# A convolution and a gated feed-forward on one core: the output projection with Wo stationary in column tiles, and the work that moves with it

## The chip, the cores and the metric

The kernel runs on one core of a Trainium2 chip. The metric is the device time of one execution in microseconds (us), as the median of several runs. Engines go by the names of the profile: PE is TensorE (matmuls; PEld its weight loads), DVE VectorE, ACT ScalarE, POOL GpSimd, SP the engine that issues DMAs here.

## The reference

The input x has 8 batches of 4096 tokens with 192 channels; `weight` has 8 heads of 7 taps. What is computed, cut to what matters:

```python
w = softmax(weight)                        # per head, over its 7 taps
x_pad = 6 zero tokens in front of each batch of x
attn[b, s, ch] = sum_k w[head(ch), k] * x_pad[b, s + k, ch]   # head(ch) = ch // 24
t = attn.reshape(32768, 192)
out = (relu(t @ w_gate) * (t @ w_val)) @ w_out                # 192 -> 1536 -> 192
```

So a causal convolution of 7 taps per channel, then a gated feed-forward. The output is 32768 x 192 in fp32; inside, the kernel works in fp16 with fp32 sums.

## The kernel before

The tokens are cut into 16 units. A unit is 1024 tokens of one batch and the same 1024 of the batch four further on, side by side as two streams (`st`), so 2048 tokens. The convolution's result of a unit is `xc`: channels on partitions (64 per stream, in 3 chunks `c`), tokens along the row, fp16.

Each turn `u` of the main loop has two stages on TensorE.

- Stage A, `gate_val` (L431), called for two windows of 512 tokens. For each of 12 slices `f` of 128 hidden channels: 6 matmuls with Wg and 6 with Wv (L444), 64 rows each, the two streams in two halves of the array's rows, 512 tokens moving. ScalarE turns the first sum into `gr` with relu (L453), VectorE multiplies it with the second out of PSUM into `hT` (L454), hidden channels on partitions.
- Stage B, `project` (L457), four times (window and stream). hT is the stationary operand, 128 tokens at a time, and Wo moves: 4 x 12 matmuls of 192 columns (L464) give 512 tokens with tokens on partitions. ScalarE copies them to `out_s` (L475), and SP stores them (L476, 384 KB).

PSUM is a rotation of four tiles `ps` of two banks each, shared by both stages: gate and value of a slice take one each, a projection takes one.

The convolution of units 0 and 1 is done by TensorE (L277, L302). For all others it runs two units ahead, on the other engines, in stage B and the following stage A. GpSimd loads x (`lane_load`, L353) and copies it in another order (`lane_turn`, L372); nine transposing DMAs on SP (L375) make `x_r`, channels on partitions. Then a unit's 1024 tokens are split in two lanes:

- VectorE's lane, 576 tokens: ScalarE makes tap 0's product `acc` (L408); VectorE adds the other six taps in 18 steps (`lane_rest`, L420), each `x_r * tap + acc`, into `xc`.
- GpSimd's lane, 448 tokens: the products of 7 taps in 3 chunks go to `prods`. ScalarE makes 16 of the 21 (L391), VectorE five after its own lane (L393, seven for unit 2). The list of VectorE's ends with chunk 2 of tap 1. GpSimd sums them in six adds over all three chunks (`add`, L397), tap 1 first; the last writes `xc`.

The order is written out by hand (`manual_schedule`): every engine runs its instructions in the order of the program. In GpSimd's queue the main loop puts, for turn `u`: the add of tap 1 for unit `u+1`, the copies for unit `u+2`, the loads for unit `u+3`, the other adds for unit `u+1`. In ScalarE's and VectorE's, stage A's work comes first, then the lanes of unit `u+2` (ScalarE's products between the evictions, four ahead of each `project`). Turn 1 is different: it also loads unit 3 and does the adds of taps 2 and 3 ahead of the copies. Turns 14 and 15 have no lanes left to start.

Of the kernel before, what the change touches and what calls it, by code (L numbers as in the profile page):

```python
# [8 lines left out]
FP = mybir.dt.float32  # L9
F16 = mybir.dt.float16  # L10
# [5 lines left out]
def kernel(  # L16
# [12 lines left out]
    nc = tc.nc  # L29

    B, S, D = x.shape
    H, KW = weight.shape
# [3 lines left out]
    NB = B // 2  # L36
    NCH = D // 64
    NBLK = D // 32
    NFF = DFF // 128
    WIN = 512  # L40
    NWIN = S // WIN
    SUB = 112
    VECTOR = [
        [(0, 5), (1, 5), (2, 5), (0, 4), (1, 4), (2, 4), (2, 1)],
        [(0, 5), (1, 5), (2, 5), (0, 6), (2, 1)],
    ]
    GSUB = 5


    UNIT = 2 * WIN  # L50
    NUNIT = NB * S // UNIT
    HALO = 64
    LDVE, LPOOL = 576, 448
    TILES = (UNIT + 2 * HALO) // 128
    TDVE = (LDVE + HALO) // 128
    GROUPS = [(0, [WIN * w + SUB * j for j in range(GSUB)]) for w in range(2)]
# [2 lines left out]

    ctx.enter_context(tc.manual_schedule())  # L60
    const = ctx.enter_context(tc.tile_pool(name="const", bufs=1))
    xpool = ctx.enter_context(tc.tile_pool(name="xpool", bufs=3))
    epool = ctx.enter_context(tc.tile_pool(name="epool", bufs=1))
    rpool = ctx.enter_context(tc.tile_pool(name="rpool", bufs=2))
    apool = ctx.enter_context(tc.tile_pool(name="apool", bufs=1))
    ypool = ctx.enter_context(tc.tile_pool(name="ypool", bufs=2))
    xcpool = ctx.enter_context(tc.tile_pool(name="xcpool", bufs=3))
    hpool = ctx.enter_context(tc.tile_pool(name="hpool", bufs=2))
    gpool = ctx.enter_context(tc.tile_pool(name="gpool", bufs=3))
    opool = ctx.enter_context(tc.tile_pool(name="opool", bufs=3))  # L70
    psum = ctx.enter_context(tc.tile_pool(name="psum", bufs=4, space=bass.MemoryType.PSUM))


    def load_x(g):


        bp, toks = GROUPS[g]
        xt = xpool.tile([128, GSUB, 2, D], F16, name="x_h")
        if toks[0] == 0:
            nc.vector.memset(xt[0:32, 0, :, :], 0.0)  # L80
        for st in range(2):
            b = bp + NB * st
            jj = int(toks[0] == 0)
            last = toks[-1] == S - SUB or toks[-1] - toks[-2] != SUB
            n_full = len(toks) - jj - int(last)
            lo = toks[jj] - PAD
            src = bass.AP(
                tensor=x.tensor,
                offset=x.offset + (b * S + lo) * D,
                ap=[[D, 128], [SUB * D, n_full], [1, D]],  # L90
            )
            nc.gpsimd.dma_start(out=xt[:, jj : jj + n_full, st, :], in_=src)  # L92
            if last:
                nc.gpsimd.dma_start(
                    out=xt[0 : SUB + PAD, len(toks) - 1, st, :],
                    in_=x[b, toks[-1] - PAD : toks[-1] + SUB, :],
                )
        for st in range(2 * int(toks[0] == 0)):
            nc.gpsimd.dma_start(
                out=xt[PAD:128, 0, st, :], in_=x[bp + NB * st, 0 : 128 - PAD, :]  # L100
            )
        return xt
# [6 lines left out]
    for half, eng in ((0, nc.sync), (1, nc.scalar)):  # L109
        eng.dma_start(  # L110
            out=wr[64 * half : 64 * half + 64],
# [12 lines left out]
    ps = psum.tile([128, 2, 512], FP, name="ps")  # L124
    for n in range(16):
        nc.tensor.matmul(  # L126
            out=ps[:, n % 2, :], lhsT=zeros[:, 0:128], rhs=zeros[:], start=True, stop=True
# [92 lines left out]
    w0 = we[:, 0:1, 0:1]  # L220
# [71 lines left out]
    def conv(g):  # L292


        xt = xts.pop(g)
        bp, toks = GROUPS[g]
        n = len(toks)
        rows = SUB + PAD
        W = 2 * n * G
        pair = [psum.tile([128, 2, 512], FP, name="ps") for _ in range(2)]  # L300
        for h, (t, bank, slot) in PLACE.items():
            nc.tensor.matmul(  # L302
                out=pair[t][0:SUB, bank, W * slot : W * (slot + 1)],
                lhsT=band(h),
                rhs=xt[0:rows, 0:n, :, G * h : G * (h + 1)],
                start=True,
                stop=True,
                skip_group_check=True,
            )
        y = ypool.tile([128, GSUB, NCH, 2, 64], F16, name="y")  # L310

        def move(copy, t, bank, i0, step_in, c, r0, step_out, width):
            src = pair[t][0:SUB, bank, 0 : 2 * W]
            dst = y[0:SUB, 0:n, 0, :, 0:1]
            copy(
                out=bass.AP(
                    tensor=dst.tensor,
                    offset=dst.offset + 128 * c + r0,
                    ap=[dst.ap[0], [step_out, 2], [NCH * 128, n], [64, 2], [1, width]],
                ),  # L320
                in_=bass.AP(
                    tensor=src.tensor,
                    offset=src.offset + i0,
                    ap=[src.ap[0], [W + step_in, 2], [2 * G, n], [G, 2], [1, width]],
                ),
            )

        move(nc.scalar.copy, 0, 0, 0, 0, 0, 0, G, G)
        move(nc.scalar.copy, 0, 1, 0, 0, 1, 8, G, G)
        move(nc.scalar.copy, 1, 0, 0, 0, 2, 16, G, G)  # L330
        move(nc.scalar.copy, 1, 1, 0, 8, 0, 48, 2 * 128 - 48, 16)
        move(nc.scalar.copy, 1, 1, 16, -16, 1, 0, 56, 8)
        for jj, t in enumerate(toks):
            nc.sync.dma_start_transpose(
                out=xc[1][:, :, t - UNIT : t - UNIT + SUB],
                in_=y[0:SUB, jj].rearrange("p c s r -> p (c s r)"),
            )
# [47 lines left out]
        return xrs[u][:, c, o : o + LDVE]  # L385

    def product(engine, u, c, k):
        out = prods[u][:, k, c, :]
        in_, scale = shifted(u, c, k, 1), tap[:, c, k : k + 1]
        if engine is nc.scalar:  # L390
            engine.activation(out=out, in_=in_, func=ACTF.Copy, scale=scale)  # L391
        else:
            engine.tensor_scalar(out=out, in0=in_, scalar1=scale, scalar2=None, op0=ALU.mult)  # L393

    def add(u, k):
        pr = prods[u]
        nc.gpsimd.tensor_tensor(  # L397
            out=pr[:, 0] if k < KW - 1 else xc[u][:, :, LDVE:UNIT],
            in0=pr[:, 0],
            in1=pr[:, k],  # L400
            op=ALU.add,
        )

    def lane_first(u):
        accs[u] = apool.tile([128, NCH, LDVE], FP, name="acc")
        xc[u] = xcpool.tile([128, NCH, UNIT], F16, name="xc")
        for c in range(NCH):
            nc.scalar.activation(  # L408
                out=accs[u][:, c, :],
                in_=shifted(u, c, 0, 0),  # L410
                func=ACTF.Copy,
                scale=tap[:, c, 0:1],
            )
        prods[u] = apool.tile([128, KW, NCH, LPOOL], FP, name="prods")

    def lane_rest(u):
        acc = accs.pop(u)
        for k in range(1, KW):
            for c in range(NCH):
                nc.vector.scalar_tensor_tensor(  # L420
                    out=xc[u][:, c, 0:LDVE] if k == KW - 1 else acc[:, c, :],
                    in0=shifted(u, c, k, 0),
                    scalar=tap[:, c, k : k + 1],
                    in1=acc[:, c, :],
                    op0=ALU.mult,
                    op1=ALU.add,
                )
        for c, k in VECTOR[u > 2]:
            product(nc.vector, u, c, k)

    def gate_val(u, w):  # L431
        h = hpool.tile([128, NFF, 2, WIN], F16, name="hT")
# [21 lines left out]
            nc.vector.tensor_tensor(out=h[:, f], in0=gr[:], in1=pss[1][:], op=ALU.mult)  # L454
        return h

    def project(bp, w, h, st, final):  # L457
        parts = [range(4)] if not final else [range(2), range(2, 3), range(3, 4)]
        row0 = (bp + NB * st) * S + WIN * w
        for n, qs in enumerate(parts):  # L460
            ps = psum.tile([128, 2, 512], FP, name="ps")
            for i, q in enumerate(qs):
                for f in range(NFF):
# [4 lines left out]
                        start=(f == 0),  # L468
                        stop=(f == NFF - 1),
                    )  # L470
            os_ = opool.tile([128, 2, 2 * D], FP, name="out_s")
            k = len(qs)
            a, m = (k + 1) // 2, min(k, 2) * D
            copy = nc.vector.tensor_copy if n == 1 else nc.scalar.copy
            copy(out=os_[:, 0:a, 0:m], in_=ps[:, 0:a, 0:m])  # L475
            (nc.scalar if n == 2 else nc.sync).dma_start(  # L476
                out=out[row0 + 128 * qs[0] : row0 + 128 * (qs[0] + k), :].rearrange(
                    "(q p) d -> p q d", p=128
                ),
                in_=os_[:, 0:a, 0:m].rearrange("p a (b d) -> p (a b) d", d=D)  # L480
                if k == 4
                else os_[:, 0, 0:m].rearrange("p (b d) -> p b d", d=D),
            )


# [3 lines left out]
    for u in range(NUNIT):  # L489
# [20 lines left out]
            xc[1] = xcpool.tile([128, NCH, UNIT], F16, name="xc")  # L510
            conv(2)
        del xc[u]
        work = [[] for _ in range(4)]
        if u + 2 < NUNIT:
            lane_first(u + 2)
            lane_rest(u + 2)
            todo = [(c, k) for k in (0, 1, 2, 3, 4, 6) for c in range(NCH)]
            todo = [ck for ck in todo if ck not in VECTOR[u > 0]]
            work = [todo[4 * i : 4 * i + 4] for i in range(4)]
        bp, w0 = u * UNIT // S, u * UNIT % S // WIN  # L520
        for i in range(4):
            for c, k in work[i]:
                product(nc.scalar, u + 2, c, k)
            project(bp, w0 + i // 2, hs[i // 2], i % 2, u == NUNIT - 1 and i == 3)
            if u == 0 and i == 0:
                conv(3)


# [28 lines left out]
```

## Time and profile before

| | |
|---|---|
| Median of 3 runs | 776.64 us (776.43 to 776.93) |
| Span of the profiled execution, first to last instruction | 774.5 us |
| Busy: PE, DVE, ACT, POOL | 765.4, 688.0, 602.3, 371.8 us |
| Granted TensorE clock | 1.000 |
| Stage A and stage B of a steady unit | 31.19 and 15.95 us |
| hT (L454) | 384 x 1221 ns |
| VectorE's lane steps (L420) | 252 x 811 ns |
| GpSimd's adds (L397) | 84 x 3.03 us |
| ScalarE's products (L391), evictions (L475) | 222 x 660 ns, 63 x 794 ns |

The durations come from one profiled execution, whose own time is its span and what lies around it. A duration is from an instruction's start to its end; neighbours on one engine overlap by some tens of nanoseconds, so their starts lie closer together than their durations say.

### The profile page before, as it was taken

Reading aid. Unit: us, or ns where it says so; the run is one execution under the profiler, and the core shown is the slowest. Engines: PE = TensorE matmul, PEld = TensorE weight load, DVE = VectorE, ACT = ScalarE, POOL = GpSimd, SP = SyncE. Lnnn points to the kernel's source line nnn. Section 1 sums busy time; section 2 is a strip of 40 time slices with the busy share of each in tenths; the row PEclk is TensorE's granted clock in tenths of the full one; section 3 lists DMA queues with packets and bytes.
Section 4 is the critical chain, followed back from the end, with each engine's and each line's share of the span. In section 5 each row is a group of like instructions: output and inputs, shape, how many; then the busy total and the mean of one; then the engine's idle time right before and its main releaser. Section 6 shows DMA issues by size and latency. Waiting matters only on the chain.

```text
span 774.5 us, 19025 instructions
## 1 busy us (share of the span) xinstructions
PE 765.4 (99%) x7952; PEld 505.7 (65%) x7952; DVE 688.0 (89%) x738; ACT 602.3 (78%) x735; POOL 371.8 (48%) x215
## 2 busy tenths in 40 slices
PE   7999999999999999999999999999999999999998
PEld 3586584855748567484764847558485674857648
DVE  6889999999999899999999999999998999986491
ACT  4798887878878787787878878788787877885572
POOL 9605929175390844809256191752908446090000
PEclk9999999999999999999999999999999999999999
DMA  9947828162291812817046281542718322100102
GB/s 113 139 69 142 90 83 93 42 100 36 82 93 60 94 24 87 87 62 114 21 89 65 84 90 42 93 42 83 92 47 93 38 87 42 63 22 22 62 1 83
DMA packets 132569, 55.62 MB, mean 72 GB/s; under 512 B 98180, under 2 KB 132484, under 8 KB 132484
## 3 DMA queue, kind: packets, MB, share of 16 engines
q1 hardware_dynamic: 90466, 38.35, 23.7%
q0 software_dynamic: 41808, 15.97, 20.4%
q8 instruction: 62, 1.02, 0.6%
q14 instruction: 23, 0.19, 0.1%
q10 hardware_dynamic: 210, 0.10, 0.0%
HBM read 31.93 MB, written 25.17 MB: 74 GB/s over the span
## 4 chain that ended last, share of the span: by engine, by line
PE 97%; DVE 1%; ACT 1%; DMA 1%; issue 1%; ACTq 0%; DVEq 0%
PE ps L444 64%; PE ps L464 33%; DMA wr<-in_weight_dram 1%; DVE hT L454 0%; ACT gr L453 0%; PE ps L302 0%; PE ps L277 0%; ACT prods L391 0%; DVE band L240 0%; DVE prod L221 0%; DVE blk L229 0%; DVE xc L287 0%; ACT out_s L475 0%; ACT we L184 0%; DVE we L181 0%
## 5 line engine op out<-in xcount | busy, mean ns | idle before, releaser
L454 DVE TENSOR_TENSOR hT<-gr,ps 128x1024 f16<-128x1024 f16 x384 | 468.6, 1221 | 62.9 <-ACT gr L453 33.6
L453 ACT ACTIVATE gr<-ps 128x1024 f16<-128x1024 f32 x384 | 392.8, 1023 | 102.9 <-PE ps L444 102.9
L397 POOL TENSOR_TENSOR prods<-prods 128x1344 f32<-128x1344 f32 x70 | 212.3, 3033 | 315.1 <-DVE prods L393 311.7
L444 PE MATMUL ps<-xc,Wv 64*128 64x512 f16 x2304 | 314.0, 376 | 1.4 <-issue 1.3
L444 PE MATMUL ps<-xc,Wg 64*128 64x512 f16 x2304 | 313.9, 376 | 0.5 <-DVE xc L287 0.3
L464 PEld LDWEIGHTS <-hT 128*128 128x128 f16 x3072 | 252.7, 98 | 6.4 <-issue 6.4
L464 PE MATMUL ps<-Wo,hT 128*128 128x192 f16 x3072 | 256.4, 246 | 0.0
L444 PEld LDWEIGHTS <-Wv 64*128 64x128 f16 x2304 | 132.0, 94 | 119.2 <-issue 2.9
L444 PEld LDWEIGHTS <-Wg 64*128 64x128 f16 x2304 | 115.2, 94 | 131.6 <-issue 3.1
L420 DVE SCALAR_TENSOR_TENSOR acc<-x_r,tap,acc 128x576 f32<-128x576 f16 x210 | 154.3, 811 | 1.8 <-ACT acc L408 1.8
L391 ACT ACTIVATE prods<-x_r,tap 128x448 f32<-128x448 f16 x222 | 130.1, 660 | 0.0
L475 ACT COPY out_s<-ps 128x768 f32<-128x768 f32 (+1 forms) x65 | 50.8, 782 | 58.3 <-PE ps L464 44.2
L353 POOL DMA_DIRECT2D x_e<-in_x_dram x56 | 45.1, 817 | 3.5 <-POOL x_p L372 2.4
L372 POOL COPY x_p<-x_e 128x1728 f16<-128x1728 f16 x28 | 44.8, 1632 | 3.2 <-DMA x_e<-in_x_dram 3.2
L397 POOL TENSOR_TENSOR xc<-prods 128x1344 f16<-128x1344 f32 x14 | 42.4, 3029 | 1.1
L420 DVE SCALAR_TENSOR_TENSOR xc<-x_r,tap,acc 128x576 f16<-128x576 f16 x42 | 31.8, 811 | 0.0
L408 ACT ACTIVATE acc<-x_r,tap 128x576 f32<-128x576 f16 x42 | 29.3, 763 | 0.0
L393 DVE TENSOR_SCALAR prods<-x_r,tap 128x448 f32<-128x448 f16 x72 | 27.3, 448 | 0.0
L475 DVE COPY out_s<-ps 128x192 f32<-128x192 f32 x1 | 0.4, 358 | 13.4 <-PE ps L464 13.4
L92 POOL DMA_DIRECT2D x_h<-in_x_dram x8 | 6.7, 843 | 0.8 <-POOLq L541 0.8
L126 PE MATMUL ps<-zeros 128*128 128x512 f16 x16 | 5.0, 482 | 1.5 <-DVE zeros L123 1.5
L277 PE MATMUL ps<-band,x_h 118*32 118x112 f16 (+7 forms) x240 | 3.5, 209 | 2.7 <-ACT band L242 2.6
(40 smaller groups left out, 49.9 us busy)
## 6 DMA issues: line engine op xcount, KB each, us to landing
out_dram<-out_s SPq DMA_DIRECT2D x63, 384.0 KB
x_e<-in_x_dram POOLq DMA_DIRECT2D x34, 192.0 KB, 6.3
x_e<-in_x_dram POOLq DMA_DIRECT2D x22, 240.0 KB, 6.2
x_r<-x_p SPq DMA_TRANSPOSE x126
x_h<-in_x_dram POOLq DMA_DIRECT2D x4, 240.0 KB, 5.7
x_h<-in_x_dram POOLq DMA_DIRECT2D x4, 192.0 KB, 5.2
Wo<-in_moe_w_out_dram POOLq DMA_DIRECT2D x1, 576.0 KB, 8.9
Wg<-in_moe_w_gate_dram POOLq DMA_DIRECT2D x3, 144.0 KB, 4.1
```

Source lines behind the costliest of these rows:

```text
L353: nc.gpsimd.dma_start(out=xe[:, j : j + n, st, :, :].rearrange("p j c r -> p j (c r)"), in_=bass.AP(tensor=x.tensor, offset=x.offset + (b ...
L372: nc.gpsimd.tensor_copy(out=xp[:, :, :, st, :], in_=xe[:, :, st, :, :])
L391: engine.activation(out=out, in_=in_, func=ACTF.Copy, scale=scale)
L393: engine.tensor_scalar(out=out, in0=in_, scalar1=scale, scalar2=None, op0=ALU.mult)
L397: nc.gpsimd.tensor_tensor(out=pr[:, 0] if k < KW - 1 else xc[u][:, :, LDVE:UNIT], in0=pr[:, 0], in1=pr[:, k], op=ALU.add,)
L408: nc.scalar.activation(out=accs[u][:, c, :], in_=shifted(u, c, 0, 0), func=ACTF.Copy, scale=tap[:, c, 0:1],)
L420: nc.vector.scalar_tensor_tensor(out=xc[u][:, c, 0:LDVE] if k == KW - 1 else acc[:, c, :], in0=shifted(u, c, k, 0), scalar=tap[:, c, k : k ...
L444: nc.tensor.matmul(out=pss[i][:, st, :], lhsT=W[64 * st : 64 * st + 64, c, 128 * f : 128 * (f + 1)], rhs=xcb[64 * st : 64 * st + 64, c, WI ...
L453: nc.scalar.activation(out=gr[:], in_=pss[0][:], func=ACTF.Relu)
L454: nc.vector.tensor_tensor(out=h[:, f], in0=gr[:], in1=pss[1][:], op=ALU.mult)
L464: nc.tensor.matmul(out=ps[:, i // 2, D * (i % 2) : D * (i % 2) + D], lhsT=h[:, f, st, 128 * q : 128 * (q + 1)], rhs=Wo[:, f, :], start=(f ...
L475: copy(out=os_[:, 0:a, 0:m], in_=ps[:, 0:a, 0:m])
```

## The change

Stage B is turned round for all units but the last. `project_columns` keeps Wo stationary, 32 output channels at a time, in four column tiles of the array; each tile has another 512 tokens of hT moving (two windows, two streams). Three passes `p` of 64 channels each fill one `ps` tile, with channels on partitions in four groups of 32. `turn_out`, on VectorE, reads it with a transpose of 32x32 blocks into the unit's `o`, tokens on partitions. `store` writes the whole unit after the third pass, in four DMAs of 384 KB on SP, 32 partitions each. The last unit keeps `project`, with slices of `o` as its buffers.

The lanes are split anew: VectorE's has 448 tokens, GpSimd's 576. VectorE makes no products any more; `lane_rest` is a generator whose 18 steps are given out as 5, 6 and 7 ahead of the three transposes. ScalarE makes 15 products, taps 1 and 2 in the first pass, 3 and 4 in the second, 0 in the third. GpSimd makes the six products of taps 5 and 6 itself, just ahead of the adds that use them. Each tap's products have a tile of their own in place of the one tile `prods`.

To make room, the first loads of x and `y` (the rearranged result of L302) lie in the two buffers that later hold `o`.

```diff
-    VECTOR = [
-        [(0, 5), (1, 5), (2, 5), (0, 4), (1, 4), (2, 4), (2, 1)],
-        [(0, 5), (1, 5), (2, 5), (0, 6), (2, 1)],
-    ]
+    ON_POOL = (5, 6)
+    STEPS = [5, 6, 7]
+    TAPS = [(1, 2), (3, 4), (0,)]
...
-    LDVE, LPOOL = 576, 448
+    LDVE, LPOOL = 448, 576
...
-    opool = ctx.enter_context(tc.tile_pool(name="opool", bufs=3))
+    opool = ctx.enter_context(tc.tile_pool(name="opool", bufs=2))
...
     def product(engine, u, c, k):
-        out = prods[u][:, k, c, :]
+        if (u, k) not in prods:
+            prods[u, k] = apool.tile([128, NCH, LPOOL], FP, name=f"prod{k}")
+        out = prods[u, k][:, c, :]
...
     def add(u, k):
-        pr = prods[u]
+        if k in ON_POOL:
+            for c in range(NCH):
+                product(nc.gpsimd, u, c, k)
+        p0 = prods[u, 0]
         nc.gpsimd.tensor_tensor(
-            out=pr[:, 0] if k < KW - 1 else xc[u][:, :, LDVE:UNIT],
-            in0=pr[:, 0],
-            in1=pr[:, k],
+            out=p0[:] if k < KW - 1 else xc[u][:, :, LDVE:UNIT],
+            in0=p0[:],
+            in1=prods.pop((u, k))[:],
             op=ALU.add,
         )
...
-        for c, k in VECTOR[u > 2]:
-            product(nc.vector, u, c, k)
+                yield
...
+    def project_columns(hs, p):
+        ps = psum.tile([128, 2, 512], FP, name="ps")
+        for b in range(2):
+            for f in range(NFF):
+                for s in range(4):
+                    nc.tensor.matmul(
+                        out=ps[32 * s : 32 * s + 32, b, :],
+                        lhsT=Wo[:, f, 64 * p + 32 * b : 64 * p + 32 * b + 32],
+                        rhs=hs[s // 2][:, f, s % 2, :],
+                        start=(f == 0),
+                        stop=(f == NFF - 1),
+                        tile_position=(0, 32 * s),
+                        skip_group_check=True,
+                    )
+        return ps
+
+    def turn_out(ps, o, p):
+        nc.vector.transpose(
+            out=o[:, :, 64 * p : 64 * p + 64].rearrange("p t (b c) -> p b t c", b=2),
+            in_=ps[:].rearrange("p b (t c) -> p b t c", c=32),
+        )
+
+    def store(o, bp, w0):
+        for s in range(4):
+            row0 = (bp + NB * (s % 2)) * S + WIN * (w0 + s // 2)
+            nc.sync.dma_start(
+                out=out[row0 : row0 + WIN, :].rearrange("(t p) d -> p t d", p=32),
+                in_=o[32 * s : 32 * s + 32],
+            )
...
+        lane = None
         if u + 2 < NUNIT:
             lane_first(u + 2)
-            lane_rest(u + 2)
-            todo = [(c, k) for k in (0, 1, 2, 3, 4, 6) for c in range(NCH)]
-            todo = [ck for ck in todo if ck not in VECTOR[u > 0]]
-            work = [todo[4 * i : 4 * i + 4] for i in range(4)]
-        bp, w0 = u * UNIT // S, u * UNIT % S // WIN
-        for i in range(4):
-            for c, k in work[i]:
-                product(nc.scalar, u + 2, c, k)
-            project(bp, w0 + i // 2, hs[i // 2], i % 2, u == NUNIT - 1 and i == 3)
-            if u == 0 and i == 0:
+            lane = lane_rest(u + 2)
+        o = opool.tile([128, UNIT // 64, D], FP, name="out_s")
+        if u == NUNIT - 1:
+            for i in range(4):
+                project(bp, w0 + i // 2, hs[i // 2], i % 2, i == 3, o[:, 4 * i : 4 * i + 4, :])
+            continue
+        for p in range(3):
+            ps = project_columns(hs, p)
+            if lane:
+                for k in TAPS[p]:
+                    for c in range(NCH):
+                        product(nc.scalar, u + 2, c, k)
+                for _ in range(STEPS[p]):
+                    next(lane)
+            turn_out(ps, o, p)
+            if u == 0 and p == 0:
                 conv(3)
+        store(o, bp, w0)
```

More of the change, by code (lines that the diff above doesn't have):

```diff
@@ L61 @@
     const = ctx.enter_context(tc.tile_pool(name="const", bufs=1))
-    xpool = ctx.enter_context(tc.tile_pool(name="xpool", bufs=3))
     epool = ctx.enter_context(tc.tile_pool(name="epool", bufs=1))
@@ L65 @@
     apool = ctx.enter_context(tc.tile_pool(name="apool", bufs=1))
-    ypool = ctx.enter_context(tc.tile_pool(name="ypool", bufs=2))
     xcpool = ctx.enter_context(tc.tile_pool(name="xcpool", bufs=3))
@@ L69, with staged @@
     gpool = ctx.enter_context(tc.tile_pool(name="gpool", bufs=3))
-    opool = ctx.enter_context(tc.tile_pool(name="opool", bufs=3))
+    opool = ctx.enter_context(tc.tile_pool(name="opool", bufs=2))
     psum = ctx.enter_context(tc.tile_pool(name="psum", bufs=4, space=bass.MemoryType.PSUM))
+    XH = GSUB * 2 * D
+    stages = [opool.tile([128, 6 * XH // 2], F16, name="out_s") for _ in range(2)]
+    def staged(i, j):
+        return stages[i][:, XH * j : XH * (j + 1)]
     def load_x(g):
         bp, toks = GROUPS[g]
-        xt = xpool.tile([128, GSUB, 2, D], F16, name="x_h")
+        xt = staged(g // 3, g % 3).rearrange("p (j s d) -> p j s d", s=2, d=D)
         if toks[0] == 0:
@@ L309, in conv @@
             )
-        y = ypool.tile([128, GSUB, NCH, 2, 64], F16, name="y")
+        y = staged(1, g - 1).rearrange("p (j c s r) -> p j c s r", c=NCH, s=2, r=64)
         def move(copy, t, bank, i0, step_in, c, r0, step_out, width):
@@ L413, in lane_first @@
             )
-        prods[u] = apool.tile([128, KW, NCH, LPOOL], FP, name="prods")
     def lane_rest(u):
@@ L455, in gate_val, with project @@
         return h
-    def project(bp, w, h, st, final):
+    def project_columns(hs, p):
[25 more added lines that the diff above has]
+            )
+    def project(bp, w, h, st, final, o):
         parts = [range(4)] if not final else [range(2), range(2, 3), range(3, 4)]
@@ L470, in project @@
                     )
-            os_ = opool.tile([128, 2, 2 * D], FP, name="out_s")
+            os_ = o[:, qs[0] : qs[0] + len(qs), :].rearrange("p (a b) d -> p a (b d)", a=(len(qs) + 1) // 2)
             k = len(qs)
@@ L474, in project @@
             copy = nc.vector.tensor_copy if n == 1 else nc.scalar.copy
-            copy(out=os_[:, 0:a, 0:m], in_=ps[:, 0:a, 0:m])
+            copy(out=os_, in_=ps[:, 0:a, 0:m])
             (nc.scalar if n == 2 else nc.sync).dma_start(
@@ L479, in project @@
                 ),
-                in_=os_[:, 0:a, 0:m].rearrange("p a (b d) -> p (a b) d", d=D)
-                if k == 4
-                else os_[:, 0, 0:m].rearrange("p (b d) -> p b d", d=D),
+                in_=o[:, qs[0] : qs[0] + k, :],
             )
@@ L512 @@
         del xc[u]
-        work = [[] for _ in range(4)]
+        bp, w0 = u * UNIT // S, u * UNIT % S // WIN
+        lane = None
         if u + 2 < NUNIT:
             lane_first(u + 2)
-            lane_rest(u + 2)
-            todo = [(c, k) for k in (0, 1, 2, 3, 4, 6) for c in range(NCH)]
-            todo = [ck for ck in todo if ck not in VECTOR[u > 0]]
-            work = [todo[4 * i : 4 * i + 4] for i in range(4)]
-        bp, w0 = u * UNIT // S, u * UNIT % S // WIN
-        for i in range(4):
-            for c, k in work[i]:
-                product(nc.scalar, u + 2, c, k)
-            project(bp, w0 + i // 2, hs[i // 2], i % 2, u == NUNIT - 1 and i == 3)
-            if u == 0 and i == 0:
+            lane = lane_rest(u + 2)
[14 more added lines that the diff above has]
+            if u == 0 and p == 0:
                 conv(3)
+        store(o, bp, w0)
 _INS = ['x', 'weight', 'moe_w_gate', 'moe_w_val', 'moe_w_out']
```

## The prediction

> **What bounds the kernel now.** I read the page first: busy time by engine, then the chain of work that ended last.
>
> ```profile
> PE 765.4 (99%) x7952; PEld 505.7 (65%) x7952; DVE 688.0 (89%) x738; ACT 602.3 (78%) x735; POOL 371.8 (48%) x215
> ...
> PE 97%; DVE 1%; ACT 1%; DMA 1%; issue 1%; ACTq 0%; DVEq 0%
> ```
>
> TensorE is busy 99% of the span and carries 97% of the chain. The chain in order of time, cut to a steady unit, splits it into the two stages:
>
> ```profile
> 299.94 31.19 PE ps L444 x288
> 331.13 15.95 PE ps L464 x192
> 347.08 3.12 PE ps L444 x27
> ```
>
> A unit is 31.19 us of gate and value (call it A) and 15.95 us of projection (B): 47.14 us, no gap between them. Time is won only by making B's matmuls cheaper, and lost by anything that makes TensorE wait. So I looked at how near the others are. The timeline of VectorE and of GpSimd around one B, which starts at 284.0 and ends at 299.94:
>
> ```profile
> 285.58 11.02 DVE L420 SCALAR_TENSOR_TENSOR acc<-x_r,tap,acc 128x576 f32<-128x576 f16 x15
> 296.52 2.27 DVE L420 SCALAR_TENSOR_TENSOR xc<-x_r,tap,acc 128x576 f16<-128x576 f16 x3
> 298.71 1.90 DVE L393 TENSOR_SCALAR prods<-x_r,tap 128x448 f32<-128x448 f16 x5
> 301.79 3.81 DVE L454 TENSOR_TENSOR hT<-gr,ps 128x1024 f16<-128x1024 f16 x3 [1.19 <-ACT gr L453]
> ```
>
> ```profile
> 276.81 3.03 POOL L397 TENSOR_TENSOR xc<-prods 128x1344 f16<-128x1344 f32 x1
> 300.78 3.03 POOL L397 TENSOR_TENSOR prods<-prods 128x1344 f32<-128x1344 f32 x1 [20.94 <-DVE prods L393]
> ```
>
> VectorE rests only 1.19 us in the unit. GpSimd waits 20.94 us, through all of B, for VectorE's last product: VectorE's lane steps (two SBUF inputs, x_r and acc) and GpSimd's adds never run at the same time. That is what the change alters.
>
> **TensorE's part.** Removed per unit: 192 matmuls of 192 columns. Added: 3 x 2 x 12 = 72 groups of four column tiles of 512 columns. The columns are the same if four run together (192 x 192 = 72 x 512). The trace has four column tiles with different weights and data, at L277:
>
> ```profile
> 21.00 1.58 PE L277 MATMUL ps<-band,x_h 118*32 118x112 f16 x120
> ```
>
> 120 matmuls in 1.58 us; by their starts, a group of four with 112 columns every 49 ns, weight loads hidden. A's pairs of 512 columns come every 215.9 ns; between the two, 0.417 ns per column and 2.3 ns per group. So a group in the new B costs 215.9 ns: 72 x 0.2159 = 15.55, plus the 0.1 us that B has today beyond 192 x 82.56 ns: 15.65 us, 0.30 less than 15.95. Units 0 to 14 change, the last keeps the old form: 15 x 0.30 = **4.5 us gained**. Bounds: 0.1 us per unit if groups of 512 columns keep the first gap of L277 (60 against 49 ns), 0.48 if nothing stands between groups (72 x 0.2135 + 0.1). The Trainium skill, TensorEngine Tiling (Array Packing), Restrictions and Gotchas, says that column tiling rules out the fast weight load; if the four loads of a group (93 ns each at L277) then came one after another, a group would take 372 ns and B 11 us more, but the 49 ns of L277 already hold four such loads, so the trace does not bear that out as a bound.
>
> B's first 12 groups now need window 1's hT, too: the last one at 11 x 0.216 = 2.4 us into B. VectorE ends it 1.65 us in (285.58 less 283.93). It is hidden by 0.7 us; if VectorE enters B later, each us beyond that is on the path.
>
> **ScalarE's part.** Removed: four evictions (0.79 us) and one product. Added width: 15 products of 576 at 0.667 us start to start (L408 has that size) and three L408 of 448 at 0.56. From 0.4 us into B: 1.7 + 10.0, done at about 12.2 us. It had 13.65 us busy there; nothing waits for it. It finishes tap 0 last, so GpSimd's first add can start at 12.2 us into B, no longer after VectorE's lane.
>
> **VectorE's part.** Removed: five products (1.90 us). The 18 lane steps shrink from 576 to 448: 0.729 us start to start less 128 x 1.04 ns (600 ns of the 729 scale with 576) = 0.596. Added: three transposes of 128x1024 from PSUM. No row has a transpose. Nearest: hT, 1.22 us for 1024 elements out of PSUM; I take that, with 0.65 (double rate) and 2.3 (half rate) as bounds. In order: 5 steps from 1.65 to 4.63; transpose 0 waits for TensorE (5.2 + 0.2), ends 6.6; 6 steps to 10.1; transpose 1 at 10.6 to 11.8; 7 steps to 15.9; transpose 2 to 17.1. Next A begins at 15.65; its second value group needs transpose 2's PSUM buffer at 15.65 + 3 x 0.65 = 17.6, and the first hT waits for its gr until 17.5. **Cover: 0.4 us.** Beyond it every us on VectorE after 11.8 stalls TensorE one for one, in 14 units. At 2.3 us per transpose the last would end at 19.9 (steps 13.4 to 17.6): 2.4 us, 34 us in all.
>
> **GpSimd's part.** Adds grow from 1344 to 1728 elements: 3.10 us start to start becomes 3.97, six of them 23.8. Copies 3.2, DMA issues 3.3. Six products of its own: no row; between the copy's rate (1632 / 1728 = 0.94 ns per element, 0.55 us) and the add's (2.3, 1.3 us): 3.3 to 8 us; I take 0.8 each, 4.8. Sum 35, from 12.2 us in one B to 47.2, the start of the next (period 46.8); the result is needed 15.6 us after that start, and tap 0's buffer by ScalarE at 10 us. It holds. SP's stores (four of 384 KB) now go out together after transpose 2, ahead of nine x_r transposes that took 12.7 us: those were issued at 16 us after B's start and now come at 20 or some 8 us later behind the store data, done by 41 of the 47 us. Hidden, too.
>
> **Where the two meet.** GpSimd's first add starts at 12.2 us while VectorE's last seven steps run from 11.8 to 15.9. What that costs the trace shows only for another pair: in the first microseconds VectorE's and GpSimd's copies of L165.
>
> ```profile
> 11.86 0.42 DVE L165 COPY Wg<-Wg 64x768 f16<-64x768 f16 x1
> 12.20 1.23 DVE L165 COPY Wv<-Wv 64x768 f16<-64x768 f16 x1
> ```
>
> ```profile
> 11.99 1.15 POOL L165 COPY Wg<-Wg 64x1152 f16<-64x1152 f16 x1
> 13.10 1.20 POOL L165 COPY Wv<-Wv 64x1152 f16<-64x1152 f16 x1
> ```
>
> The same VectorE copy takes 0.42 us, or 1.23 when it comes behind a GpSimd copy: it ends 0.28 after that one ended (13.14). Against hT, which reads one SBUF input, GpSimd costs nothing (1214 to 1223 ns throughout). A lane step stands between these: two SBUF inputs. Bounds per unit: nothing; or the add and both copies each hold VectorE off in full, 3.97 + 1.6 + 1.6 = 7.2. I take one full blocking by the add. The second GpSimd copy above ran beside VectorE's and lost 50 ns (1.20 against 1.15), so I leave the copies free. Then two steps are done at 12.9, VectorE stands to 16.9, five steps to 19.9, transpose 2 to 21.1: 3.5 us past 17.6. Times 14: 49 us. The Trainium skill, SBUF — State Buffer, Who interferes with whom, states that a VectorE instruction with two SBUF inputs contends with a GpSimd one that reads SBUF, as an exclusive lock held for the whole instruction. No run here shows that for these two instructions; by it the sum would be the third rival's.
>
> **Sum.** Span 774.5, time 776.64 (median of three): 2.1 us lie around the span. 774.5 - 4.5 + 49 + 2.1 = **821 us**.
>
> **Rivals.**
> 1. No collision that matters: the steps are served as if alone, or GpSimd waits and has slack. For it: GpSimd has 11 us and more to spare, hT shows no loss. Against: the blocked copy, and a cover of only 0.4 us. 774.5 - 4.5 + 2.1 = 772; faster. It decides if the steps beside an add stay at 0.68 us each.
> 2. VectorE's stream keeps the way and the add waits to 15.9: GpSimd's tail then reaches some 3.5 us into the next B, and the last add holds the first steps there to about 3.8 instead of 1.65. Transpose 2 ends 1 to 2 us late: 772 + 14 x 1 to 2 = 786 to 800.
> 3. Every GpSimd instruction that reads SBUF takes its turn: 7.2 - 0.4 = 6.8 us in units 0 to 13, and about twice that in units 12 and 13, whose next unit has no loads between the copies and the adds: 772 + 12 x 6.8 + 2 x 14 = 882. This is the rule of the page named above, to the letter.
> 4. Transposes at half rate without a collision: 772 + 34 = 806.
> 5. Column tiles that don't run together at 512 columns: up to four times B. Against it stands the 49 ns at L277; chance 2 in 100, over 1300 us.
>
> **How the numbers follow.** Forecast (one blocking, anything between 800 and 862 counted to it) 0.33; rival 1 0.33, of which 0.02 within 0.2% because the TensorE gain comes out below 1.5 us; rival 2 0.08; rival 3 0.18; rival 4 0.06; rival 5 0.02. Forecast and rival 1 stand level; I name the forecast, since the cases that share its sign hold 0.67 and it lies in their middle. Its own range is 800 to 862. The range that holds 8 in 10 goes from 769 (rival 1 with the upper bound of the gain, 15 x 0.48 = 7.2 instead of 4.5) to 862 and leaves out rivals 3 and 5. 0.2%, 1.6 us, is about what a measurement of this kernel can tell from no change. Faster 0.31, same 0.02, slower 0.67.
>
> **What would show it.** In the new chain: L444 stays 31.2 us per unit; the new projection 15.6. If I am right, VectorE's lane steps have a longest duration of some 4.6 us against a median near 0.68, the wait of ps at L444 for the transpose shows some 3.5 us 14 times, and GpSimd's add is near 3.9. Wrong on the collision: all steps within a few ns of each other and no wait of L444 on VectorE. Wrong on the transpose: its mean far from 1.22. Wrong on TensorE: the new groups not 216 ns apart.

## The result and the profile after

The changed kernel takes 904.84 us (median of four runs) against 776.78 before: ratio 1.1648, 95% interval 1.1629 to 1.1667. The forecast was slower, 821 us, in a range of 769 to 862; the time lies above the range. The profiled execution has a span of 902.2 us.

In the changed kernel's rows L450 is stage A's matmuls, L470 the new projection, L427 VectorE's lane steps, L484 its transposes, L405 GpSimd's adds, L375 its copies, L356 its loads of x, L396 and L398 the products. Its page, busy time, granted clock in 40 slices, and the chain that ended last:

```profile
PE 789.6 (88%) x9392; PEld 402.2 (45%) x9392; DVE 792.2 (88%) x711; ACT 568.9 (63%) x663; POOL 597.4 (66%) x299
...
PEclk9997989989899898989989899898999969969999
...
PE 75%; DVE 19%; issue 4%; DMA 0%; ACT 0%; DVEq 0%
```

TensorE is no longer on the whole chain: 19% of it is VectorE, and the clock, at 9 throughout before, drops once in each unit from 1 to 14. The chain in order of time, its short pieces left out, shows where, for one unit whose projection begins at 325.20:

```profile
325.20 10.50 PE ps L470 x192
336.98 4.85 DVE acc L427 x3
341.83 1.83 issue
343.65 2.04 DVE acc L427
346.21 1.27 DVE xc L427 x2
348.69 31.13 PE ps L450 x270
379.82 10.50 PE ps L470 x192
```

After two of the three passes the chain leaves TensorE for VectorE's lane steps (L427) and comes back to TensorE only at 348.69. The unit lasts 379.82 - 325.20 = 54.62 us; it was 47.14 before. The timelines of VectorE and GpSimd in that stretch:

```profile
336.90 8.79 DVE L427 SCALAR_TENSOR_TENSOR acc<-x_r,tap,acc 128x448 f32<-128x448 f16 x4
345.61 1.86 DVE L427 SCALAR_TENSOR_TENSOR xc<-x_r,tap,acc 128x448 f16<-128x448 f16 x3
347.40 1.24 DVE L484 STREAM_TRANSPOSE out_s<-ps 128x1024 f32<-128x1024 f32 x1
```

```profile
337.42 3.86 POOL L405 TENSOR_TENSOR prod<-prod,prod 128x1728 f32<-128x1728 f32 x1 [12.15 <-ACT prod L396]
341.23 3.98 POOL L375 COPY x_p<-x_e 128x1728 f16<-128x1728 f16 x2
345.51 3.33 POOL L356 DMA_DIRECT2D x_e<-in_x_dram  x4 [0.30 <-POOL x_p L375]
```

Beside the add and the copies, four steps take 8.79 us; beside the DMA issues of the loads, three take 1.86. By their own rows in the trace, the step that meets the add lasts 4.31 us (337.46 to 341.77; the add ends at 341.29), and the two that meet the copies 2.04 each. The last transpose, due at 15.9 us into the projection, starts at 22.2 (347.40 - 325.20). Over the whole run:

```profile
L427 DVE SCALAR_TENSOR_TENSOR acc<-x_r,tap,acc x210: 642/680/4319, 49.4 to 793.2; 128x448 f32<-128x448 f16 x105
L427 DVE SCALAR_TENSOR_TENSOR xc<-x_r,tap,acc x42: 671/672/7150, 62.2 to 802.6; 128x448 f16<-128x448 f16 x42
```

(minimum, median, longest in ns.) The step of 7.15 us stands apart. It starts at 66.99, beside the first of four DMA issues (66.54 to 69.80), and ends at 74.14, after the add behind them (69.79 to 73.65): the issues did not let it through there. What TensorE does meanwhile, from its timeline and from the table by stretches (length, busy time of PE, PEld, DVE, ACT and POOL, each with its count, then the granted clock, DMA share and GB/s):

```profile
348.69 1.47 PE L450 MATMUL ps<-xc,Wv 64*128 64x512 f16 x6 [5.79 <-DVE out_s L484]
349.92 1.51 PE L450 MATMUL ps<-xc,Wg 64*128 64x512 f16 x6
```

```profile
340.79:348.69 7.90, 2.11 (x23) 0.88 (x19) 7.90 (x8) 2.05 (x2) 7.60 (x7) 0.80 0.23 22
348.69:353.00 4.31, 4.31 (x24) 1.87 (x25) 2.55 (x3) 1.02 (x1) 4.23 (x3) 0.57 1.38 172
```

It stands 5.79 us, and then eight pairs of matmuls come 427 ns apart instead of 216. The granted clock is 0.50 from 345.6 to 352.4, so from the middle of the wait to the end of these pairs.

What the change brought on TensorE itself is there as well: a projection takes 15.65 us where nothing disturbs it (the last but one, 836.42 to 852.07), A 31.19.

### The profile page after: what moved, and what is told of

It reads as the page before. It is cut to its first block, busy times and chain, and to the rows that moved or that the text cites. A ratio compares the mean times of both kernels' runs of the same rounds, so it can differ in the third digit from the quotient of the medians.

```text
span 902.2 us, 21815 instructions
## 1 busy us (share of the span) xinstructions
PE 789.6 (88%) x9392; PEld 402.2 (45%) x9392; DVE 792.2 (88%) x711; ACT 568.9 (63%) x663; POOL 597.4 (66%) x299
## 4 chain that ended last, share of the span: by engine, by line
PE 75%; DVE 19%; issue 4%; DMA 0%; ACT 0%; DVEq 0%
PE ps L450 55%; PE ps L470 18%; DVE acc L427 11%; DVE xc L427 4%; DVE out_s L484 4%; PE ps L506 2%; DMA wr<-in_weight_dram 0%; DVE hT L460 0%; ACT gr L459 0%; PE ps L305 0%; PE ps L280 0%; DVE band L243 0%; DVE prod L224 0%; DVE blk L232 0%; ACT out_s L517 0%
## 5 line engine op out<-in xcount | busy, mean ns | idle before, releaser
L450 PE MATMUL ps<-xc,Wv 64*128 64x512 f16 x2304 | 334.4, 393 | 105.4 <-DVE out_s L484 103.9
L405 POOL TENSOR_TENSOR prod<-prod,prod 128x1728 f32<-128x1728 f32 x70 | 271.7, 3881 | 212.1 <-ACT prod L396 208.7
L450 PE MATMUL ps<-xc,Wg 64*128 64x512 f16 x2304 | 327.2, 386 | 0.2 <-DVE hT L460 0.2
L450 PEld LDWEIGHTS <-Wv 64*128 64x128 f16 x2304 | 139.0, 97 | 230.9 <-issue 125.1
L470 PE MATMUL ps<-hT,Wo 128*32 128x512 f16 x4320 | 236.0, 379 | 0.0
L427 DVE SCALAR_TENSOR_TENSOR acc<-x_r,tap,acc 128x448 f32<-128x448 f16 x210 | 214.8, 1089 | 1.6 <-ACT acc L416 1.6
L450 PEld LDWEIGHTS <-Wg 64*128 64x128 f16 x2304 | 127.6, 97 | 136.6 <-issue 24.1
L470 PEld LDWEIGHTS <-Wo 128*32 128x32 f16 x4320 | 114.1, 97 | 120.3 <-issue 6.3
L398 POOL TENSOR_SCALAR prod<-x_r,tap 128x576 f32<-128x576 f16 x84 | 144.3, 1731 | 0.0
L396 ACT ACTIVATE prod<-x_r,tap 128x576 f32<-128x576 f16 x210 | 141.4, 765 | 0.0
L484 DVE STREAM_TRANSPOSE out_s<-ps 128x1024 f32<-128x1024 f32 x45 | 56.1, 1246 | 27.0 <-PE ps L470 27.0
L375 POOL COPY x_p<-x_e 128x1728 f16<-128x1728 f16 x28 | 54.3, 1961 | 3.6 <-DMA x_e<-in_x_dram 3.6
L405 POOL TENSOR_TENSOR xc<-prod,prod 128x1728 f16<-128x1728 f32 x14 | 53.8, 3842 | 1.2
L427 DVE SCALAR_TENSOR_TENSOR xc<-x_r,tap,acc 128x448 f16<-128x448 f16 x42 | 50.9, 1263 | 0.0
L356 POOL DMA_DIRECT2D x_e<-in_x_dram x56 | 46.5, 845 | 3.5 <-POOL x_p L375 2.4
L506 PE MATMUL ps<-Wo,hT 128*128 128x192 f16 x192 | 16.0, 246 | 0.0
L506 PEld LDWEIGHTS <-hT 128*128 128x128 f16 x192 | 15.8, 98 | 0.4 <-issue 0.4
```

Of the source, the lines that this page charges most:

```text
L356: nc.gpsimd.dma_start(out=xe[:, j : j + n, st, :, :].rearrange("p j c r -> p j (c r)"), in_=bass.AP(tensor=x.tensor, offset=x.offset + (b ...
L375: nc.gpsimd.tensor_copy(out=xp[:, :, :, st, :], in_=xe[:, :, st, :, :])
L405: nc.gpsimd.tensor_tensor(out=p0[:] if k < KW - 1 else xc[u][:, :, LDVE:UNIT], in0=p0[:], in1=prods.pop((u, k))[:], op=ALU.add,)
L427: nc.vector.scalar_tensor_tensor(out=xc[u][:, c, 0:LDVE] if k == KW - 1 else acc[:, c, :], in0=shifted(u, c, k, 0), scalar=tap[:, c, k : k ...
L450: nc.tensor.matmul(out=pss[i][:, st, :], lhsT=W[64 * st : 64 * st + 64, c, 128 * f : 128 * (f + 1)], rhs=xcb[64 * st : 64 * st + 64, c, WI ...
L470: nc.tensor.matmul(out=ps[32 * s : 32 * s + 32, b, :], lhsT=Wo[:, f, 64 * p + 32 * b : 64 * p + 32 * b + 32], rhs=hs[s // 2][:, f, s % 2, ...
```

## The experiments

**All products on ScalarE.** One part of the change is undone: GpSimd makes no products. ScalarE then ends tap 0 four us later.

```diff
-    ON_POOL = (5, 6)
+    ON_POOL = ()
-    TAPS = [(1, 2), (3, 4), (0,)]
+    TAPS = [(1, 2), (3, 4), (5, 6, 0)]
```

> The changed kernel with GpSimd's six products moved to ScalarE (ON_POOL empty, TAPS = [(1, 2), (3, 4), (5, 6, 0)]); nothing else differs. ScalarE then ends tap 0 at about 0.4 + 1.7 + 21 x 0.667 = 16.1 us into the projection, when VectorE's 18 lane steps are done (15.9). Theory (a lane step and a GpSimd instruction that reads SBUF exclude each other): no step beside a GpSimd add or copy, all steps near 0.68 us, no wait of TensorE for the last transpose, full clock; the projection's 0.3 us gain per unit is left: 772 us, at most 775. Rival A (the transposes, the column tiles or the stores burst cost the time): they are all still there, so near 900. Rival B (GpSimd's queue is simply too long, 41 us): shorter by 10 us, so faster than 905 as well; it differs from the theory in the next run.

780.55 us, ratio 1.005 (1.0037 to 1.0063): rival A falls, as column tiles, transposes and the burst of stores are all there. It is not the 772, at most 775, of the theory. From unit 3 on every unit lasts 46.84 us; units 1 and 2, which are set up differently, last 48.42 and 54.12, 8.9 us more together. In this stretch two steps still meet an add (3.37 and 4.26 us), and TensorE waits 4.44 us for a transpose.

**The same work, tap 0 earlier.** Only the order of ScalarE's products differs from the run above.

```diff
-    TAPS = [(1, 2), (3, 4), (5, 6, 0)]
+    TAPS = [(1, 2), (0, 3), (4, 5, 6)]
```

> As the run with all products on ScalarE, but TAPS = [(1, 2), (0, 3), (4, 5, 6)]: the same instructions on every engine, only ScalarE makes tap 0 at about 8 us into the projection instead of 16, so GpSimd's first add can start there. Theory: GpSimd's add and its two copies fall among the lane steps again, and each holds one step up for its whole length; the second and third transposes come late, TensorE waits some 9 us per unit and loses another 2 to a low clock: 930 to 970 us. Rival B (GpSimd's length is the cause): starting earlier can only help, 772 us.

1135.75 us, in one run. Rival B falls: the same instructions on each engine, and letting GpSimd start 8 us sooner costs 355 us. The size was underrated (930 to 970 were expected): most units last 73 to 75 us. GpSimd's DMA issues fell on the second transpose this time, so that GpSimd had little but adds left for the seven steps behind it. The first of them runs free beside a DMA issue (0.64 us); the second starts beside the third of the four issues and ends 5.79 us later, after the add that follows them; four more last 4.24 us each, beside an add; the last is free. VectorE and TensorE in that unit:

```profile
427.19 14.66 DVE L427 SCALAR_TENSOR_TENSOR acc<-x_r,tap,acc 128x448 f32<-128x448 f16 x4
441.78 9.00 DVE L427 SCALAR_TENSOR_TENSOR xc<-x_r,tap,acc 128x448 f16<-128x448 f16 x3
```

```profile
451.99 1.46 PE L450 MATMUL ps<-xc,Wv 64*128 64x512 f16 x6 [23.85 <-DVE out_s L484]
```

Seven steps, 4.2 us of work, take 23.6 us, and TensorE waits 23.85 for the transpose behind them.

**Steps with one SBUF input.** The changed kernel as it is, except for one operand of the steps.

```diff
-                    in0=shifted(u, c, k, 0),
+                    in0=seen[0][:, 0, 0:LDVE],
...
+            seen[0] = pss[1]
...
             turn_out(ps, o, p)
+            seen[0] = ps
```

`seen[0]` is an older sum of the matmuls, in PSUM. The kernel leaves out x_r in the steps, so VectorE's lane holds no convolution; the number and size of the steps stay.

> The changed kernel with one operand of VectorE's lane steps read from PSUM (an old sum of the matmuls) instead of x_r in SBUF; the lane's result is therefore meaningless, its count and sizes are the same. GpSimd's work, its start at 12.2 us into the projection and all orders stay. Theory: with a single SBUF input the steps don't exclude GpSimd, all take near 0.7 us beside its adds, and the time is about 772 to 776 us. Rival C (the steps wait for GpSimd through a semaphore or through the order, or GpSimd slows whatever VectorE does): near 905 us still.

771.34 us, in one run. GpSimd's add starts at the same point among the last steps and its last one beside the first steps of the next unit; its queue is as long. The steps don't notice. The line of the steps over the run, and GpSimd beside steps at 340.88 to 345.0 in its timeline:

```profile
L427 DVE SCALAR_TENSOR_TENSOR acc<-ps,tap,acc x210: 642/674/684, 49.3 to 670.5; 128x448 f32<-128x448 f32 x105
```

```profile
341.41 3.89 POOL L405 TENSOR_TENSOR prod<-prod,prod 128x1728 f32<-128x1728 f32 x1 [6.39 <-ACT prod L396]
```

The longest step is 684 ns. The order of the instructions is the same, and the steps run free beside GpSimd's adds, so rival C falls. What makes a step wait is its second input from SBUF. (The edit also takes away the steps' need to wait for x_r, and makes the operand fp32. But in the changed kernel VectorE sat idle before a step only once, 1.6 us for ScalarE's product, so no such wait explains the long steps.) This is also about what the change is worth without the collision: 771.3 us, 5.4 less than the 776.74 of the kernel before beside it.

**The wait filled.** TensorE multiplies zeros while it would wait.

```diff
+            if 1 <= u < NUNIT - 1 and w == 0 and f == 1:
+                for n in range(26):
+                    nc.tensor.matmul(
+                        out=pss[0][:, n % 2, :], lhsT=zeros[:, 0:128], rhs=zeros[:], start=True, stop=True
+                    )
```

> The changed kernel with 26 matmuls of zeros put ahead of the second slice's gate matmuls in the first window of units 1 to 14 (5.6 us), into the PSUM tile that those matmuls overwrite: TensorE works through the time in which it would wait for the third transpose. Everything else stays. Theory of the low clock (the eight slow pairs after the wait, 427 ns apart instead of 216, come from TensorE's rest of 5.8 us): with no rest of that length the pairs stay at 216 ns, granted clock 1.00, and the run is 14 x 1.7 = 24 us shorter than the changed kernel, near 881 us; the steps are held up as before. Rival (the pairs are slow because the stores and loads burst just then, 172 GB/s): the burst stays, the pairs stay slow, 905 us.

883.43 us in one run, 21 less than the changed kernel. Steady units last 52.81 instead of 54.62, and the pairs behind the filled stretch are back at 216 ns:

```profile
333.95 5.79 PE L449 MATMUL ps<-zeros 128*128 128x512 f16 x26
339.67 0.82 PE L455 MATMUL ps<-xc,Wg 64*128 64x512 f16 x6
340.46 0.82 PE L455 MATMUL ps<-xc,Wv 64*128 64x512 f16 x6
```

The burst is still there, 180 GB/s from 339.67 to 344.0 at a granted clock of 1.00. So the slow pairs come from the rest, not from the burst: 1.81 us per unit. Three longer waits were not filled to the end (22.8 us in all), hence a mean clock of 0.986 and not 1.

**The kernel before, its first add let go early.** In both lists ScalarE and VectorE exchange two products.

```diff
-        [(0, 5), (1, 5), (2, 5), (0, 4), (1, 4), (2, 4), (2, 1)],
-        [(0, 5), (1, 5), (2, 5), (0, 6), (2, 1)],
+        [(0, 5), (1, 5), (2, 5), (0, 4), (1, 4), (2, 4), (2, 6)],
+        [(0, 5), (1, 5), (2, 5), (0, 6), (2, 6)],
```

> The kernel before, with two products exchanged in both lists: ScalarE makes chunk 2 of tap 1, VectorE chunk 2 of tap 6 in its place. Work per engine is the same; old projection, no transposes, old lanes. GpSimd's first add no longer waits for VectorE's last product and can start at about 7 us into the projection. Theory: the add and the two copies hold lane steps up, 6 us and more per unit, VectorE comes late to hT and TensorE waits, with a low clock behind it: 860 us or more. Rival A (what is new in the projection costs the time, not the meeting of steps and adds): 777 us.

999.50 us, in one run. Nothing of the new projection is in it, and it is slower than the changed kernel. In a unit, the 15 steps that took 11.02 us take 26.50 beside GpSimd:

```profile
354.81 26.50 DVE L420 SCALAR_TENSOR_TENSOR acc<-x_r,tap,acc 128x576 f32<-128x576 f16 x15
```

```profile
359.82 3.07 POOL L397 TENSOR_TENSOR prods<-prods 128x1344 f32<-128x1344 f32 x1 [32.33 <-ACT prods L391]
362.84 4.26 POOL L372 COPY x_p<-x_e 128x1728 f16<-128x1728 f16 x2
```

Not only steps wait. VectorE's products, with one input from SBUF, take 0.44 us each; the last of the five that end its list (from 384.87) meets an add and takes 3.20. So it goes in six of the units.

```profile
383.42 4.65 DVE L393 TENSOR_SCALAR prods<-x_r,tap 128x448 f32<-128x448 f16 x5
384.73 3.09 POOL L397 TENSOR_TENSOR prods<-prods 128x1344 f32<-128x1344 f32 x1 [4.04 <-DVE prods L393]
```

GpSimd's 21 us of rest in the kernel before were not slack: the product of tap 1 at the end of VectorE's list kept the two apart.

**Only the start held.** GpSimd keeps its six products; VectorE makes one of tap 0's behind the third transpose.

```diff
-                    for c in range(NCH):
+                    for c in range(NCH - int(k == 0)):
...
             turn_out(ps, o, p)
+            if lane and p == 2:
+                product(nc.vector, u + 2, 2, 0)
```

> The changed kernel, with chunk 2 of tap 0's products made by VectorE behind its third transpose instead of by ScalarE: GpSimd's first add can't start before the lane steps are done. GpSimd keeps its six own products, so it works 41 us from about 17.7 us into the projection and reaches 12 us into the next one (period 46.8). Theory (a step and a GpSimd instruction that reads SBUF exclude each other, wherever): the last six steps go free, the first ones are held up by the tail instead; the two kinds of work don't fit beside each other in a unit; 870 to 905 us. Rival (only the first add's start among the last steps is harmful): 772 us.

830.55 us, in one run. The rival falls (772), but the forecast of 870 to 905 is missed as well: most units last 51 us, not 54. The tail does reach into the next projection, but GpSimd's own products do little harm there. The steps that met three products, 357.41 to 362.53, and the one that met the last add:

```profile
L427 DVE SCALAR_TENSOR_TENSOR acc<-x_r,tap,acc x5: 671/1116/1182, 357.5 to 360.8; 128x448 f32<-128x448 f16 x5
```

```profile
363.12 3.87 DVE L427 SCALAR_TENSOR_TENSOR acc<-x_r,tap,acc 128x448 f32<-128x448 f16 x1
```

A product of 1.71 us holds one step up for some 0.5 us, the add holds one until it ends. The two kinds of work don't fit beside each other in a unit with six products on GpSimd, and most units pay about one add and the slow pairs behind the wait. The waits of TensorE are shorter here, and they show how long a rest has to be to bring slow pairs:

```profile
683.13 1.47 PE L450 MATMUL ps<-xc,Wv 64*128 64x512 f16 x6 [2.42 <-DVE out_s L484]
733.55 0.82 PE L450 MATMUL ps<-xc,Wv 64*128 64x512 f16 x6 [1.81 <-DVE out_s L484]
```

Behind the wait of 2.42 us the pairs are slow (six matmuls in 1.47 us), behind that of 1.81 they are not (0.82). All eleven waits from 2.42 to 4.48 us have slow pairs behind them, the two of 1.46 and 1.81 us have none.

**Steps 6, 6, 6.** All products on ScalarE, `STEPS = [6, 6, 6]`.

> As the run with all products on ScalarE, with the steps given out 6, 6, 6 instead of 5, 6, 7. Theory: the last step ends 0.6 us earlier, so the last transpose waits for TensorE alone and the next stage has 0.4 us of cover more. Where the run before it keeps every wait hidden, the two are the same within 1 us, 772; if that one loses 0.2 to 0.5 us per unit at the last transpose, this one gains it, 3 to 7 us.

779.97 us, ratio 1.0043 (1.003 to 1.0057), against 780.55: within 1 us, so the steps' split hid nothing any more. Units 1 and 2 still last 48.44 and 53.80.

**Both losses at the start mended.** On top of that:

```diff
         if u == 1:
-            lane_load(3)
             add(2, 2)
...
             xts[3] = load_x(3)
-        if 0 < u < NUNIT - 3:
+            lane_load(3)
+        if 1 < u < NUNIT - 3:
...
             add(u + 1, KW - 1)
+        if u == 1:
+            lane_load(4)
...
-                    for c in range(NCH):
+                    for c in range(1 if u == 0 and k == 0 else NCH):
                         product(nc.scalar, u + 2, c, k)
...
             turn_out(ps, o, p)
+            for c in range(1, NCH if u == 0 and p == 2 else 1):
+                product(nc.vector, 2, c, 0)
```

> A version meant to beat both: all products on ScalarE, steps 6, 6, 6, and the two losses mended that this left at the start. There, unit 1's GpSimd queue ran to 101.1 us while the first lane steps began at 98.2 (a step held up for 3.4 us, and one more by the next add, TensorE waiting 4.4 us and then at a low clock), and ScalarE came 1.4 us late from unit 0. Edits: unit 3's loads go ahead of unit 1's adds, unit 4's loads behind them, and two of unit 2's products go to VectorE. Theory: no step over 0.8 us anywhere, no wait of TensorE for a transpose, 770 to 773 us against 776.7. If other waits at the start take their place, 775 to 779.

773.28 us (five runs) against 776.58 for the kernel before, measured beside it: ratio 0.9956, interval 0.9942 to 0.997. It is 0.4% faster than the kernel before, and 0.3 us above the 770 to 773 that were expected. Its page and its line of steps:

```profile
PE 97%; DVE 1%; DMA 1%; issue 0%; ACT 0%; DVEq 0%
```

```profile
L427 DVE SCALAR_TENSOR_TENSOR acc<-x_r,tap,acc x210: 642/677/685, 49.7 to 670.5; 128x448 f32<-128x448 f16 x105
```

No step over 685 ns, clock 1.00, units of 46.84 us from the second on. The profiled span of 770.2 us, that of the fastest of the five, is 4.3 below that of before; the medians are 3.3 apart.

## Why the prediction was right or wrong

The sign was right, by chances of 0.67 to 0.31, and so was the mechanism for the add. Most terms held: A at 31.19; the projection at 15.65, as forecast; ScalarE's tap 0 ready, and so GpSimd's first add, 12.2 us into the projection (337.42 - 325.20); a transpose at 1.25 us against 1.22; no loss to weight loads; stores and x_r transposes hidden. Rival 1's 772 is what the kernel takes with the collision taken out (771.3). Rival 2 falls because GpSimd did not give way, rivals 4 and 5 with the transpose's 1.25 us and the groups' 217 ns.

The step that failed is the price of the meeting: "I take one full blocking by the add", with the copies free. Measured in a steady unit: the add holds one step to 4.31 us, each copy one step to 2.04 instead of 0.68. 3.6 + 2 x 1.4 = 6.4 us, and a wait of 5.79 us in place of 3.5. The reason given for leaving the copies free does not carry. The 50 ns are what a GpSimd copy lost when it came second; what the step had to fear was the other order, and for that the shown rows had a GpSimd copy holding VectorE's from 0.42 to 1.23 us. That price was given to the add and not to the copies. The rule of the Trainium skill, SBUF — State Buffer, Who interferes with whom, was the better guide here, and I had given the rival built on it 0.18. For adds and copies the trace agrees with it; for GpSimd's products it does not, as the 0.5 us of 1.71 show. The kernel before speaks plainly once one asks why GpSimd waits for the last product; I had read 21 us of rest and not what they were for.

A second term was missing altogether: the clock. The sum let TensorE go on at full pace after each wait. Filling the wait gave 1.81 us per steady unit back, 21 us in all. The Trainium skill, TensorE: Matmul & The Clock Gate, Part 1, says that the clock halves after an idle window of about 3.4 us and needs about as long a busy one to return; eight pairs at 427 ns after a rest of 5.79 us (3.4 us at a granted clock near a half) agree with it. The run with only the start held differs from it: there rests of 2.42 us and more already brought slow pairs. So the forecast's own wait of 3.5 us should have carried the term, and rival 3's 6.8; rival 2's 1 to 2 us hardly, as rests of 1.46 and 1.81 us brought none.

With both, the time closes (a unit counted from the start of its stage A): 771.3 without the collision; 11 steady units at 54.62 instead of 46.84 give 85.6; unit 1 takes 58.45, 11.6 more; the two projections before the units that issue no loads between copies and adds cost 18.2 and 17.0 (65.08 and 63.83), as rival 3 had it with "about twice that". Sum 903.7, measured 904.84. Rival 3 alone, 882, lacked the clock.

A third error did no harm: GpSimd's products, taken at 0.8 us with a bound of 1.3, take 1.72. The time came out of GpSimd's rest, 12 us of which was left per unit, but it decides the run with only the start held. Above all the range was too low at the top: its 862 is added up nowhere, and it left out rival 3, the one case that priced every add and copy as the shown row has it. Two small readings don't come out either, and nothing hung on them: 11 ns more in each of 72 groups would be 0.8 us, a loss and not a gain of 0.1 per unit; and VectorE's rest in a unit was 2.9 us in all (284.00 to 331.13), of which the 1.19 are the longest piece.

## What to carry to other kernels

An engine's long rest may be what keeps its instructions from meeting another's; before moving work into it, look at which instructions of the two never overlap in the trace, and test the overlap with the cheapest edit (here, two entries of a list). A lane step with two SBUF inputs beside GpSimd should be priced at the whole length of each GpSimd add or copy that it can meet, once for each turn; one of the two inputs from PSUM took the price away here. A product of VectorE's out of SBUF paid it as well (3.20 us for 0.44). A stall of TensorE of 2.4 us or more should be priced with the slow matmuls behind it, 1.3 to 2.9 us each time in the run with only the start held.

## What the runs showed of the hardware

- GpSimd's instructions differ in how they hold a step up: an add of 3.85 us and a copy of 1.6 us for their whole length, a product (one fp16 input, fp32 output) of 1.71 us for 0.5. Why the product differs is open. Adds and copies on one side and steps on the other take turns, one of each; copies are held as well: 2.01 us beside steps, 1.62 without.
- Most steps run free beside GpSimd's DMA issues (672 ns in a steady unit), but some that start beside one wait until the add behind the issues ends: 7.15 us once in the changed kernel, 5.79 in the unit shown of the run with tap 0 earlier, 5.26 in the unit shown of the kernel before with its add let go early (from 369.08). No run shows why.
- GpSimd's product takes 1.72 us for 576 elements, 3.0 ns each, more than its two-input add (3.85 us for 1728, 2.2 ns).
- VectorE's transpose of 128x1024 fp32 out of PSUM takes 1.25 us, about a product of that shape out of PSUM (hT, 1.22).
- Four column tiles of 128x32 weights with different data keep the pace of one matmul of 512 columns: 288 in 15.65 us, 217 ns per group of four.
